# A fused scan and feed-forward kernel: wide decays, low words on ScalarE, scan products in two pieces

## The chip, the cores and the metric

The kernel runs on one core of one Trainium2 chip. The metric is device time in microseconds (us) of that core for one execution. In the profile the core's engines are PE (TensorE, matrix products; PEld is its loading of weights), DVE (VectorE), ACT (ScalarE), POOL (GpSimd) and SP (SyncE, which here issues nearly all DMAs). Each engine has its own list of instructions, and engines wait for each other through semaphores.

## The reference

A Mamba-2 scan is followed by a feed-forward layer with ELU. The scan's inputs are x (4 batches, 8 heads, 768 tokens, 32 channels), a decay `a` per token and head, and B and C (16 states per token and head). Cut to one chunk of tokens, it is:

```python
cum = np.cumsum(np.log(np.clip(a, 1e-06, 1.0)), axis=-1)
L = np.exp(cum[:, :, :, None] - cum[:, :, None, :]) * causal
M = np.einsum('bhin,bhjn->bhij', C, B) * L
y = np.einsum('bhij,bhjd->bhid', M, x) + np.einsum('bhin,bhnd->bhid', C, state) * np.exp(cum)[..., None]
state = np.exp(la.sum(-1))[..., None, None] * state + np.sum(Bx_decayed_to_the_end, axis=2)
```

The 8 heads of 32 channels then stand side by side as 3072 tokens of 256 features, and

```python
h = x @ w_in                      # 256 -> 2048
g = np.where(h > 0.0, h, np.exp(np.minimum(h, 0.0)) - 1.0)
out = g @ w_out                   # 2048 -> 256
```

`w_in` and `w_out` arrive as 64-bit floats. The kernel reads them as pairs of 32-bit words and makes 32-bit floats of them itself, with integer and float operations on the words.

## The kernel before, in words

**Tiling.** The tokens are cut into 12 blocks of 256 tokens (`BLK`), three per batch. A block has two tiles of 128 tokens (u), each of two chunks of 64 (v); the scan works on chunks of 64 instead of 32, which gives the same y. Blocks are counted 0 to 11 in the order of the work; blocks 0 and 1 are the first blocks of two batches, 2 and 3 the next ones of the same batches, and so on.

**The scan of a block.** `spread_cum` (by a DMA that reads each row for 64 partitions) lays the running sums of the log decays into a tile L of 128 x 1024. `decay_of(n, h)` makes the decays of one head of it: two ACT exponentials of 128x64 (line 521), whose bias is a column of `ncum`, minus the running sum of the row's token. After every fourth head two POOL instructions (line 526, `affine_select`) put zeros above the diagonal. `decay(n, q)` is two heads. `scores` makes the products of B and C in four PSUM tiles, `weigh` multiplies one of them by L into M on DVE, `sums` makes the chunks' contributions to the state, `states` runs the recurrence on DVE and spreads each state with its head mask on POOL (Sx). `across` multiplies the states by C into four PSUM tiles y, `inside` adds the products of M and x (line 634), and the results are copied to SBUF as yT (line 651, ACT).

**The words of the weights.** `pieces` 0 to 7 are w_in, 8 to 15 are w_out, each 128x512 32-bit results. `w_take` issues an absolute value of the high word (`w_abs`, ACT, line 196), the low word (`w_low`, line 205 on ACT or 209 on DVE) and the sign (`w_sign`, DVE). `w_give` issues two DVE operations that clip and join (`w_high`, lines 231 and 238) and a POOL sum that puts high and low together (`w_sum`, line 248). Nobody may use the piece before that sum.

**The first layer.** For blocks 0 and 1, and for the first half of the columns of blocks 2 and 3, it is made by `l1` in 32-bit floats (line 666): one PSUM tile for 256 columns, and `elu` evicts it with two ACT instructions (679, 686) and one on DVE (688), which makes g. From block 2's ninth column group on, `l1_words` (line 786) multiplies words instead: y is split into a high word y1, a rest y0 and a combination of both, w likewise (`words_of_w`, `low_of_w` on POOL, `words_of_y`, `both_of_y`). A group of 128 columns of two blocks takes three pairs of products, into a tile `high` and a tile `both`. ACT scales `both` into e (line 790), DVE joins it to `high` (793), `begin_end` makes the exponential on ACT (799, 800) and `end_words` g on DVE (807).

**The second layer.** For blocks 0 and 1 it is `l2` (line 826), which accumulates 16 products of 128 rows in one output tile; from block 2 on it is `second` (line 901), which multiplies two blocks at once with seven products instead of eight, on sums and differences of quarters that POOL and DVE make. `second` is a generator: `l2s(k)` in the schedule issues its next k pieces, of two products each.

**What sets the order.** The kernel runs with a schedule by hand: each engine's instructions stand in the order in which Python issues them. PSUM tiles of the pool "a" come round in a ring of seven, so a product that takes a tile waits until the one seven tiles earlier has been read.

After a start-up for blocks 0 and 1, a loop of twelve steps `s` (from line 1089) makes the first layer of block 1 and the rest of block 0. On the side it makes the decays of block 2 (one head in each of steps 0 to 7, line 1093), a weight piece in each odd step (5 to 10), block 2's turns of B and C, its scores and state products in step 7, block 3's first four heads of decay in step 9 (1125), and block 2's `inside` in step 10.

A second loop of eight steps `j` (from 1170) makes the first layer of blocks 2 and 3 (four tiles each), the second layer of block 0, pieces 11 to 15 (in all steps but 1, so 15 in step 5), the other decays of block 3 (step 0), its scores, states and `inside` (steps 1 to 3), and in step 4 the words of y of blocks 2 and 3.

A third loop of eight (i) goes on with the word products of blocks 2 and 3 and with `l2` of block 1; in its step 4 stand `across` and `inside` of blocks 4 and 5. The last loop takes two blocks at a time (n = 4 to 10): sixteen word products with their share of `second` for the two blocks before, and the scan of the two blocks after, whose `inside` stands at k = 13 and whose words of y stand at k = 15. DMAs of the weights stand on SP's queue in the order of use; the loads of pieces 11 to 15 are issued in the twelve-step loop.

Of the kernel before, what the change touches and what calls it, by code (L numbers as in the profile page):

```python
# [14 lines left out]
ALU = mybir.AluOpType  # L15
ACT = mybir.ActivationFunctionType

P = 128
Q = 64
# [13 lines left out]
def kernel(  # L33
# [73 lines left out]
    def rows_of(n):  # L107
        b, g = place(n)
        return slice(NG * NH * b + g, NG * NH * (b + 1), NG)
# [403 lines left out]
    def decay(n, q):  # L513

        decay_of(n, 2 * q)
        decay_of(n, 2 * q + 1)

    def decay_of(n, h):
        L, row = st[n]["L"], rows_of(n).start + NG * h
        for u in range(2):  # L520
            nc.scalar.activation(  # L521
                L[:, h, u], L[:, h, u], ACT.Exp, bias=ncum[:, u, row:row + 1])
        if h % 4 == 3:
            for v in range(2):
                part = L[Q * v:Q * v + Q, h - 3:h + 1]
                nc.gpsimd.affine_select(  # L526
                    out=part, in_=part, pattern=[[0, 4], [0, 2], [1, Q]],
                    compare_op=ALU.is_ge, fill=0.0, base=0, channel_multiplier=-1)

# [89 lines left out]
                            tile_position=(32 * q, col), skip_group_check=True)  # L621
        return y

    def inside(y, *ns):

        for t in range(2):
            for at, n in enumerate(ns):
                s = st[n]
                for u in range(2):
                    for v in range(2):  # L630
                        toks = slice(Q * v, Q * v + Q)
                        for q in range(4):
                            h, col = 4 * t + q, (D * q + shift(n, v)) % P
                            nc.tensor.matmul(  # L634
                                out=y[t][v][col:col + D, at, u],
                                lhsT=s["x"][toks, u, D * h:D * (h + 1)],
                                rhs=s["M"][h // 2][toks, u, h % 2], start=False, stop=True,
                                tile_position=(Q * v, col), skip_group_check=True)
            n = ns[0]
            if n // 2 not in yT:  # L640
                yT[n // 2] = ffn.tile([P, KC, 2, 2, P], F32, tag="yT", name="yT")
            out = yT[n // 2][:, t, n % 2:n % 2 + len(ns)]
            for v in range(2):
                k = shift(n, v)
                for at in (0, k) if k else (0,):
                    count, src = P - k, (at + k) % P
                    to, src = out[at:at + count, :, :, Q * v:Q * v + Q], y[t][v][src:src + count]
                    if t and n == 1:
                        nc.vector.tensor_copy(to, src)
                    else:  # L650
                        nc.scalar.copy(out=to, in_=src)
        for n in ns:
            st.pop(n)


    g_of = {}
# [92 lines left out]
    def words_of_y(n):  # L749

        y = yT[n // 2].rearrange("p k b u i -> p k (b u i)")
        y1 = conv.tile([P, KC, 2 * BLK], F32R, tag="y1", name="y1", bufs=1)
        y0 = conv.tile([P, KC, 2 * BLK], F32R, tag="y0", name="y0", bufs=1)
        nc.scalar.activation(y1[:, 1], y[:, 1], ACT.Copy, scale=NEAR / WORD)
        if n == 4:
            nc.scalar.activation(y1[:, 0], y[:, 0], ACT.Copy, scale=NEAR / WORD)
        else:
            nc.vector.tensor_scalar(
                out=y1[:, 0], in0=y[:, 0], scalar1=NEAR / WORD, scalar2=None, op0=ALU.mult)
        for k in range(KC):  # L760
            nc.vector.scalar_tensor_tensor(  # L761
                out=y0[:, k], in0=y1[:, k].bitcast(F32), scalar=WORD, in1=y[:, k],
                op0=ALU.mult, op1=ALU.subtract)
        y_words[n] = y1, y0
# [8 lines left out]
                in1=y[:, k], op0=ALU.mult, op1=ALU.add)  # L773
        y_words[n] = y1, y0, both

    def l1_words(n, m):

        cols = slice(m % 2 * P, (m % 2 + 1) * P)
        w, w0 = k_words[m // 2]
        w1, both_w, w0 = w[:, 0, :, cols], w[:, 1, :, cols], w0[:, :, cols]  # L780
        y1, y0, both_y = y_words[n]
        high, both = psum([P, 2 * BLK], "ps_h"), psum([P, 2 * BLK], "ps_w")
        passes = [(high, w1, y1), (high, w0, y0), (both, both_w, both_y)]
        for ps, lhs, rhs in passes if n > 2 and m == 0 else passes[2:] + passes[:2]:
            for k in range(KC):
                nc.tensor.matmul(  # L786
                    out=ps, lhsT=lhs[:, k], rhs=rhs[:, k], start=k == 0 and lhs is not w0,
                    stop=k == KC - 1 and lhs is not w1)
        e = ffn.tile([P, 2 * BLK], F32, tag="e", name="e", bufs=2)
        nc.scalar.activation(e, both, ACT.Copy, scale=WORD)  # L790
        if late:
            end_words()
        nc.vector.scalar_tensor_tensor(  # L793
            out=high, in0=high, scalar=WORD - 1.0, in1=e, op0=ALU.mult, op1=ALU.add)
        late.append((n, m, high, e))
# [167 lines left out]
    def w_take(i, low):  # L963

        w_abs(i)
        w_low(i, low)
        w_sign(i)
# [121 lines left out]
    for s, (n, i) in enumerate((  # L1089
            (1, 0), (1, 1), (1, 2), (0, 4), (1, 3), (0, 5), (1, 4), (0, 6), (1, 5), (0, 7),  # L1090
            (1, 6), (1, 7))):
        l1(n, i, parts=2 if s < 2 else 1)
        if s < 8:
            decay_of(2, s)
        if s == 7:
            st[0] = kept
            scores(2)
            sums(2, 0, pool=p_o, tag="o", parts=(None, last))
            weigh(2, 0)
            weigh(2, 1)  # L1100
        if s % 2 == 1 and todo < 11:
            w_take(todo, nc.vector)
            w_give(todo)
            w_load(todo + 6)
            todo += 1
        if s in (1, 3):
            load_bc(3, us=(s // 2,))
        if s == 9:
            write_flat(0)
        if s == 4:  # L1110
            scaled(2, nc.gpsimd)
        if s == 5:
            turn(2)
            turn_exp(2)
        if s == 4:
            load_x(3)
            spread_exp(3)
        if s == 8:
            weigh(2, 2)
            weigh(2, 3)  # L1120
            states(0, last)
            st.pop(0)
            states(2)
        if s == 9:
            decay(3, 0)
            decay(3, 1)
        if s == 10:
            spread_cum(4)
            inside(across(2), 2)
        if len(lag) > 1:  # L1130
            elu()
# [38 lines left out]
    for j in range(2 * DIRECT):  # L1170
        n, i = 2 + j // DIRECT, j % DIRECT
        if j < 7:
            l2(0, j)
        piece = todo < len(pieces) and j != 1
        if j == 0:
            elu()
        if piece:
            w_take(todo, nc.vector)
        l1(n, i)
        if j == 7:  # L1180
            l2(0, j)
        if j == 0:
            scaled(3, nc.gpsimd)
            turn(3)
            elu()
            turn_exp(3)
        if piece:
            w_give(todo)
            todo += 1
        while lag:  # L1190
            elu()
        if j == 0:
            decay(3, 2)
            decay(3, 3)
        if j == 1:
            scores(3)
            sums(3)
            for q in range(4):
                weigh(3, q)
        if j == 2:  # L1200
            states(3)
        if j == 3:
            inside(across(3), 3)
        if j == 4:
            words_of_y(2)
        if j == 4:
            words_of_w(4)
        if j == 5:
            low_of_w(4)
        if j == 5:  # L1210
            both_of_y(2)
        scan_ahead(j)
        if j == 3:
            s_out[:] = weight_sums()
        if j == 6:
            differences(0, 4)
        if j == 7:
            words_of_w(5)
    for j in range(8, 16):
# [32 lines left out]
        if i == 3:  # L1252
            l2(1, 3)
        if i == 4:
            l2(1, 4)
            y = across(4, 5)
            inside(y, 4, 5)
        if i == 5:
            l2(1, 5)
        if i in (0, 1, 3, 4):  # L1260
# [37 lines left out]
    for n in range(4, NP, 2):  # L1298
# [3 lines left out]
        def l2s(count):  # L1302
            for _ in range(count):
                next(steps)

        for k in range(16):
            l1_words(n, k)
            if m and k == 15:
                words_of_y(m)
            turn_step(n, k // 2 * 2 + 1, k % 2)  # L1310
            if n == 4 and k == 0:
                decay(6, 1)
# [9 lines left out]
            if not m:  # L1322
                l2s(4 if k % 2 else 3)
                continue
            l2s((3 + (n == 4), 3 - (n == 4), 3, 3, 3, 3, 3, 3, 4, 5, 2, 2, 3, 1, 3, 0)[k])
            if k == 9:
                scores(m, m + 1)
                sums(m, m + 1)
# [5 lines left out]
                states(m + 1)  # L1334
            if k == 13:
                y = across(m, m + 1)
                l2s(2)
                inside(y, m, m + 1)
        if m:
            l2s(4)  # L1340
            both_of_y(m)
# [38 lines left out]
```

## Time and profile before

| | |
|---|---|
| three runs | 352.52, 352.54, 353.02 us; median 352.54 |
| the profiled execution | span 351.1 us, 9871 instructions, TensorE clock 1.0 |
| PE | 339.3 us busy (97%) |
| DVE | 259.8 us (74%) |
| ACT | 234.8 us (67%) |
| POOL | 217.2 us (62%) |
| ACT from 30 to 60 us | 9.34, 9.13 and 9.46 of each 10 us |

Of the profiled execution its span is known, from its first to its last instruction; the runs' times also hold what lies around it. Busy shares are means over the whole span, and the stages differ: until 28 us the pipeline fills; from 28 to 83 us stand the loops of twelve and eight steps; from 118 us on the last loop repeats with a period of about 53 us. A row of the timeline gives start, length, engine, line, operation, result and operands, how many instructions were joined to the row, and in brackets how long the engine had been idle and who ended that. A row of a group gives, after its count, busy time and mean length in ns, and the idle time before. PE's lengths are modelled and overlap, so its waits are best seen in the distance from one start to the next.

### The profile page before, as it was taken

How to read it: one execution, taken by the hardware profiler on the slowest of the kernel's cores; microseconds unless marked ns; L12 is line 12 of the kernel's file. 1: busy time of each engine (PE TensorE's matmuls, PEld its weight loads, DVE VectorE, ACT ScalarE, POOL GpSimd, SP SyncE). 2: the span in 40 equal slices, each digit the busy share in tenths (PEclk: the TensorE clock that was granted, in tenths of full speed). 3: DMA queues.
4: the chain of work that ended last, by engine and by line, in shares of the span. 5: the costliest groups of instructions: out<-in, count | busy, mean ns of one | idle time of the engine just before them, and what ended most of it. 6: DMA issues, size and time to landing. Idle time of an engine off the chain costs nothing.

```text
span 351.1 us, 9871 instructions
## 1 busy us (share of the span) xinstructions
PE 339.3 (97%) x3878; PEld 297.3 (85%) x3878; DVE 259.8 (74%) x515; ACT 234.8 (67%) x537; POOL 217.2 (62%) x338
## 2 busy tenths in 40 slices
PE   8789999998999999999999999999999999999995
PEld 5469888887777899988889988889988999999995
DVE  4798988879997899875878775878775766665332
ACT  5688989597748888657599447599457466565000
POOL 5563554566999599975196764196754164455760
PEclk9999999999999999999999999999999999999999
DMA  8887998370270421170421170320000100001002
GB/s 143 220 226 150 315 190 239 89 138 31 65 142 7 94 59 31 12 155 4 106 60 32 13 153 5 93 45 2 2 0 5 62 0 3 0 2 60 3 0 62
DMA packets 72727, 26.49 MB, mean 75 GB/s; under 512 B 57768, under 2 KB 67560, under 8 KB 72680
## 3 DMA queue, kind: packets, MB, share of 16 engines
q1 hardware_dynamic: 70360, 25.60, 31.7%
q8 instruction: 30, 0.49, 0.6%
q10 hardware_dynamic: 2320, 0.26, 0.5%
q14 instruction: 17, 0.14, 0.1%
HBM read 22.51 MB, written 3.34 MB: 74 GB/s over the span
## 4 chain that ended last, share of the span: by engine, by line
PE 82%; SPq 4%; DMA 4%; DVE 3%; POOL 3%; ACT 2%; issue 2%; POOLq 0%; DVEq 0%
PE ps_o L901 35%; PE ps_h L786 18%; PE ps_w L786 9%; PE ps_h L666 8%; PE ps_o L826 4%; PE ps_y L634 2%; DMA w<-in_moe_w_in_dram 2%; DMA xr<-in_x_dram 2%; PE ps_g L541 2%; SPq L178 2%; PE ps_y L616 1%; PE ps_st L571 1%; POOL L L526 1%; POOL w L842 1%; DVE y L761 1%
## 5 line engine op out<-in xcount | busy, mean ns | idle before, releaser
L901 PEld LDWEIGHTS ps_o<-w_out,g 128*128 128x128 f32 x640 | 78.5, 191 | 3.4
L901 PE MATMUL ps_o<-w_out,g 128*128 128x128 f32 x640 | 80.1, 275 | 0.0
L799 ACT ACTIVATE e<-ps_h 128x512 f32<-128x512 f32 x72 | 43.0, 597 | 46.8 <-DVE ps_h L793 46.8
L807 DVE SCALAR_TENSOR_TENSOR g<-e,ps_h 128x512 f32<-128x512 f32 x72 | 49.3, 685 | 32.4 <-ACT e L800 32.1
L842 POOL TENSOR_TENSOR g<-g 128x256 f32<-128x256 f32 x36 | 26.6, 739 | 58.1 <-DVE g L807 58.0
L793 DVE SCALAR_TENSOR_TENSOR ps_h<-ps_h,e 128x512 f32<-128x512 f32 x72 | 50.0, 695 | 12.0 <-ACT e L790 9.1
L790 ACT ACTIVATE e<-ps_w 128x512 f32<-128x512 f32 x72 | 42.3, 587 | 19.8 <-PE ps_w L786 19.7
L786 PE MATMUL ps_w<-y_both,w_words 128*128 128x512 f32 x144 | 52.0, 439 | 0.1
L666 PE MATMUL ps_h<-yT,w_in 128*128 128x256 f32 (+1 forms) x208 | 45.1, 367 | 3.5 <-POOL w_in L248 3.5
L800 ACT ACTIVATE e<-e 128x512 f32<-128x512 f32 x72 | 45.5, 632 | 2.3
L786 PE MATMUL ps_h<-y,w_words 128*128 128x512 f32 x144 | 45.6, 398 | 0.0
L786 PE MATMUL ps_h<-y,w 128*128 128x512 f32 x144 | 44.9, 392 | 0.2 <-POOL w L842 0.2
L666 PEld LDWEIGHTS ps_h<-yT,w_in 128*128 128x128 f32 x208 | 36.3, 190 | 9.4 <-POOL w_in L248 4.6
L521 ACT ACTIVATE L<-L,ncum 128x64 f32<-128x64 f32 x160 | 42.2, 337 | 0.2
L901 PE MATMUL ps_o<-w_sum,g 128*128 128x128 f32 x304 | 38.4, 275 | 0.0
L901 PEld LDWEIGHTS ps_o<-w_sum,g 128*128 128x128 f32 x304 | 37.0, 192 | 1.3 <-ACT e L790 0.2
L526 POOL TENSOR_SCALAR_AFFINE_SELECT L<-L 64x512 f32<-64x512 f32 x40 | 29.3, 733 | 9.6 <-ACT L L521 8.3
L786 PEld LDWEIGHTS ps_h<-y,w 128*128 128x128 f32 x144 | 27.0, 188 | 7.0 <-POOL w L842 0.7
L786 PEld LDWEIGHTS ps_h<-y,w_words 128*128 128x128 f32 x144 | 26.7, 188 | 6.2 <-issue 0.5
L842 POOL TENSOR_TENSOR g<-t,g 128x256 f32<-128x256 f32 x40 | 28.2, 736 | 5.8 <-PE ps_o L901 5.7
L826 PE MATMUL ps_o<-w_out,g 128*128 128x256 f32 x128 | 30.5, 382 | 1.0 <-POOL w_out L248 1.0
L842 POOL TENSOR_TENSOR g<-g,t 128x256 f32<-128x256 f32 x40 | 28.7, 753 | 0.2
(133 smaller groups left out, 536.7 us busy)
## 6 DMA issues: line engine op xcount, KB each, us to landing
L<-flat SPq DMA_DIRECT2D x20, 256.0 KB
w<-in_moe_w_out_dram SPq DMA_DIRECT2D x8, 512.0 KB
w<-in_moe_w_in_dram SPq DMA_DIRECT2D x7, 512.0 KB
xr<-in_x_dram SPq DMA_DIRECT2D x24, 128.0 KB
out_dram<-c_sum SPq DMA_DIRECT2D x9, 256.0 KB
bc<-in_B_dram SPq DMA_DIRECT2D x24, 64.0 KB
bc<-in_C_dram SPq DMA_DIRECT2D x22, 64.0 KB
ec<-flat_exp SPq DMA_DIRECT2D x10, 128.0 KB
```

The lines of the kernel that those rows point to most:

```text
L521: nc.scalar.activation(L[:, h, u], L[:, h, u], ACT.Exp, bias=ncum[:, u, row:row + 1])
L526: nc.gpsimd.affine_select(out=part, in_=part, pattern=[[0, 4], [0, 2], [1, Q]], compare_op=ALU.is_ge, fill=0.0, base=0, channel_multiplier=-1)
L666: nc.tensor.matmul(out=ps[:, j, toks], lhsT=w_in[i][:, k, j * P:(j + 1) * P], rhs=yT[n // 2][:, k, n % 2].rearrange("p u i -> p (u i)")[:, ...
L786: nc.tensor.matmul(out=ps, lhsT=lhs[:, k], rhs=rhs[:, k], start=k == 0 and lhs is not w0, stop=k == KC - 1 and lhs is not w1)
L790: nc.scalar.activation(e, both, ACT.Copy, scale=WORD)
L793: nc.vector.scalar_tensor_tensor(out=high, in0=high, scalar=WORD - 1.0, in1=e, op0=ALU.mult, op1=ALU.add)
L799: nc.scalar.activation(e, high, ACT.Relu, scale=-1.0)
L800: nc.scalar.activation(e, e, ACT.Exp, scale=-1.0)
L807: nc.vector.scalar_tensor_tensor(out=g_of[n, m].rearrange("p b i -> p (b i)"), in0=e, scalar=1.0, in1=h, op0=ALU.subtract, op1=ALU.max)
L826: nc.tensor.matmul(out=o_of[n][:, ts], lhsT=g_of[n, j][:, m % 2, ts * P:(ts + 1) * P], rhs=w_out[:, m], start=(m == 0 and ts == 0), stop=( ...
L842: nc.gpsimd.tensor_tensor(out=out, in0=in0, in1=in1, op=ALU.subtract)
L901: nc.tensor.matmul(out=ps[:, ts], lhsT=b[:, ts * P:(ts + 1) * P], rhs=a[:, i], start=(i == chunk[0] and ts == 0), stop=(i == chunk[-1]), s ...
```

## The change

1. `w_take` makes the low word on ACT, not DVE, for pieces 5 to 15.
2. A new function `decay_half` makes four heads of a block's decays at once: one POOL sum of L and ncum over 128x512, one ACT exponential over 128x512, then the two masks, which now stand in a function `mask`. Blocks 2 and 3 use it: block 2 in steps 2 and 4 of the twelve-step loop, block 3 in step 9 and in step 0 of the eight-step loop. The other blocks keep `decay_of`.
3. Piece 15 moves from step 5 of the eight-step loop to the end of step 4, ahead of the words of y.
4. `words_of_y` makes both halves of y1 on ACT for blocks 2 and 4 (before: for 4 alone). For blocks 2 and 3 the first word group (m = 8) multiplies `high` before `both`. In the last loop the words of y are issued between the products of group 15 and that group's eviction.
5. `inside` can be issued in two pieces, and two or four products of the second layer are put ahead of and between them.

```diff
+    def decay_half(n, half, eng=nc.gpsimd):
+        heads = slice(4 * half, 4 * half + 4)
+        part = st[n]["L"][:, heads]
+        rows = rows_of(n)
+        rows = slice(rows.start + 4 * NG * half, rows.start + 4 * NG * (half + 1), NG)
+        eng.tensor_tensor(
+            out=part, in0=part,
+            in1=ncum[:, :, rows].rearrange("p u h -> p h u").unsqueeze(3).to_broadcast(
+                [P, 4, 2, Q]), op=ALU.add)
+        nc.scalar.activation(part, part, ACT.Exp)
+        mask(n, half)
...
-    def inside(y, *ns):
-        for t in range(2):
+    def inside(y, *ns, ts=(0, 1)):
+        for t in ts:
...
-        if n == 4:
+        if n < 6:
             nc.scalar.activation(y1[:, 0], y[:, 0], ACT.Copy, scale=NEAR / WORD)
...
-        for ps, lhs, rhs in passes if n > 2 and m == 0 else passes[2:] + passes[:2]:
+        for ps, lhs, rhs in passes if m == (8 if n == 2 else 0) else passes[2:] + passes[:2]:
...
+        if between:
+            words_of_y(between)
         e = ffn.tile([P, 2 * BLK], F32, tag="e", name="e", bufs=2)
         nc.scalar.activation(e, both, ACT.Copy, scale=WORD)
...
-        if s < 8:
-            decay_of(2, s)
+        if s in (2, 4):
+            decay_half(2, s // 2 - 1)
...
         if s % 2 == 1 and todo < 11:
-            w_take(todo, nc.vector)
+            w_take(todo, nc.scalar)
...
         if s == 9:
-            decay(3, 0)
-            decay(3, 1)
+            decay_half(3, 0)
...
         if piece:
-            w_take(todo, nc.vector)
+            w_take(todo, nc.scalar)
...
+        if j == 4:
+            w_take(todo, nc.scalar)
+            w_give(todo)
+            todo += 1
         if j == 0:
-            decay(3, 2)
-            decay(3, 3)
+            decay_half(3, 1)
...
         if i == 4:
-            l2(1, 4)
             y = across(4, 5)
-            inside(y, 4, 5)
+            l2(1, 4, half=0)
+            inside(y, 4, 5, ts=(0,))
+            l2(1, 4, half=1)
+            inside(y, 4, 5, ts=(1,))
...
-            l1_words(n, k)
-            if m and k == 15:
-                words_of_y(m)
+            l1_words(n, k, between=m if k == 15 else None)
...
-            l2s((3 + (n == 4), 3 - (n == 4), 3, 3, 3, 3, 3, 3, 4, 5, 2, 2, 3, 1, 3, 0)[k])
+            l2s((3 + (n == 4), 3 - (n == 4), 3, 3, 3, 3, 3, 3, 4, 5, 2, 2, 3, 1, 2, 0)[k])
...
                 y = across(m, m + 1)
+                l2s(1)
+                inside(y, m, m + 1, ts=(0,))
                 l2s(2)
-                inside(y, m, m + 1)
+                inside(y, m, m + 1, ts=(1,))
```

More of the change, by code (lines that the diff above doesn't have):

```diff
@@ L516, in decay, with mask @@
         decay_of(n, 2 * q + 1)
+    def decay_half(n, half, eng=nc.gpsimd):
[9 more added lines that the diff above has]
+        mask(n, half)
+    def mask(n, half):
+        for v in range(2):
+            part = st[n]["L"][Q * v:Q * v + Q, 4 * half:4 * half + 4]
+            nc.gpsimd.affine_select(
+                out=part, in_=part, pattern=[[0, 4], [0, 2], [1, Q]],
+                compare_op=ALU.is_ge, fill=0.0, base=0, channel_multiplier=-1)
     def decay_of(n, h):
@@ L523, in decay_of @@
         if h % 4 == 3:
[L524 to L528, printed above, removed]
+            mask(n, h // 4)
     def scores(*ns):
@@ L651, in inside @@
                         nc.scalar.copy(out=to, in_=src)
-        for n in ns:
-            st.pop(n)
+        if 1 in ts:
+            for n in ns:
+                st.pop(n)
     g_of = {}
@@ L774, in both_of_y, with l1_words @@
         y_words[n] = y1, y0, both
-    def l1_words(n, m):
+    def l1_words(n, m, between=None):
         cols = slice(m % 2 * P, (m % 2 + 1) * P)
```

## The prediction

> **What bounds the kernel now.** I read the page's engine table first, then the chain that ended last, then the table of 10 us windows, then the timeline from 24 to 97 us, where the change has nearly all its edits.
>
> ```profile
> span 351.1 us, 9871 instructions
> PE 339.3 (97%) x3878; PEld 297.3 (85%) x3878; DVE 259.8 (74%) x515; ACT 234.8 (67%) x537; POOL 217.2 (62%) x338
> PE 82%; SPq 4%; DMA 4%; DVE 3%; POOL 3%; ACT 2%; issue 2%; POOLq 0%; DVEq 0%
> ```
>
> The windows (us, length, then PE, PEld, DVE, ACT and POOL busy with their counts, clock, DMA share, GB/s):
>
> ```profile
> 30.00:40.00 10.00, 10.00 (x58) 9.05 (x58) 8.96 (x17) 9.34 (x23) 5.21 (x6) 1.00 0.93 276
> 40.00:50.00 10.00, 9.99 (x168) 8.08 (x173) 9.19 (x23) 9.13 (x24) 5.35 (x9) 1.00 0.94 217
> 50.00:60.00 10.00, 10.00 (x116) 8.53 (x105) 8.31 (x16) 9.46 (x25) 4.61 (x5) 1.00 1.03 262
> ```
>
> TensorE (PE) is the bound: 97% busy, 82% of the chain, full clock. So an engine beside it matters only where PE waits for it, and a wait put on PE stays in the time. Between 30 and 60 us ScalarE (ACT) is busy 9.1 to 9.5 us of 10, GpSimd (POOL) about half. The averages of the whole span (ACT 67%) hide that.
>
> ```profile
> 31.47 0.69 DVE L238 SCALAR_TENSOR_TENSOR mag<-mag,sgn 128x512 uint32<-128x512 uint32 x1
> 32.24 1.27 POOL L248 TENSOR_TENSOR w_in<-mag,w_in 128x512 uint32<-128x512 uint32 x1 [1.79 <-DMA xr<-in_x_dram]
> 32.50 0.57 ACT L679 ACTIVATE e<-ps_h 128x512 f32<-128x512 f32 x1
> ...
> 46.13 2.02 ACT L521 ACTIVATE L<-L,ncum 128x64 f32<-128x64 f32 x8
> 50.37 0.69 DVE L238 SCALAR_TENSOR_TENSOR mag<-mag,sgn 128x512 uint32<-128x512 uint32 x1
> 50.31 1.66 ACT L651 COPY yT<-ps_y 128x128 f32<-128x128 f32 x6 [1.01 <-PE ps_y L634]
> 50.63 1.99 PE L666 MATMUL ps_h<-yT,w_in 128*128 128x256 f32 x8
> 51.14 1.26 POOL L248 TENSOR_TENSOR w_out<-mag,w_out 128x512 uint32<-128x512 uint32 x1 [2.04 <-DVE mag L238]
> 52.35 1.40 POOL L526 TENSOR_SCALAR_AFFINE_SELECT L<-L 64x512 f32<-64x512 f32 x2
> ...
> 83.05 1.99 PE L826 MATMUL ps_o<-w_out,g 128*128 128x256 f32 x8 [1.01 <-POOL w_out L248]
> 105.93 0.74 PE L634 MATMUL ps_y<-M,xr 64*32 64x64 f32 x51 [0.41 <-issue]
> 160.89 0.46 PE L634 MATMUL ps_y<-M,xr 64*32 64x64 f32 x31 [0.32 <-issue]
> ```
>
> See three things. The exponentials of block 3 end on ACT at 48.15, but their mask (L526) starts at 52.35: it stands on POOL behind a weight sum (L248) that waits for DVE's L238. PE takes up the last product of block 1 at 50.63, as soon as ACT has copied the first y out of PSUM (50.31). And PE breaks off inside the scan products (L634) for 0.3 to 0.4 us, with no releaser shown.
>
> **Step 1, low words by ScalarE.** Eleven pieces (5 to 15): DVE loses 11 x 0.43 = 4.7 us, ACT gains 11 x 0.66 = 7.3 (0.67 is the same-sized L196; L205 itself shows 0.75 under overlap; back to back I add 0.6). No PE instruction waits for it directly.
>
> **Step 2, wide decays.** For blocks 2 and 3 ACT loses 32 exponentials at 2.02/8 = 0.25, 8.1 us, and gains four of 128x512 at 0.63 (L686's row), 2.5 us. POOL gains four 128x512 sums L + ncum. No row shows that one: between 0.74 (L842, 128x256) and 1.64 (twice L408's 0.82, a 128x256 sum with a broadcast operand); I take 1.28, L248's, which has its size. Beside step 1, ACT's work from 28 to 57 us is nearly unchanged. But each exponential now waits for its sum on POOL, and each sum stands behind the weight sum just issued, which waits for three DVE operations, of which the first waits for ACT's own absolute value. Behind the waiting exponential on ACT stand the eviction of the next first-layer tile (L679, L686) and the copies of y, and PE waits for these.
>
> A, block 2's first half: L238 ends at 32.16 less a low of 0.6, 31.6; weight sum 32.9, sum 34.2, exponential 34.85. The next eviction starts there, not at 32.50: +2.35. PE has PSUM tiles in hand and does not feel it. B, its second half: eviction, absolute value and low word 37.25, DVE's three 38.1, weight sum 39.4, sum 40.7, exponential 41.3; the eviction that began at 36.33 begins at 41.3. After the copy of the turned B (44.05) and two evictions (45.25, 46.45), DVE ends its two products g at 46.25 and 47.1. Scores and state products of block 2 reuse those PSUM tiles: state products start at 47.1, not 43.34, **+3.8**.
>
> C, block 3's first half: in the trace L238 ends 7.7 us after the state products began (51.06 - 43.34); less two lows (0.8) that is 54.0 now. Weight sum 55.3, sum 56.6, exponential 57.2, eviction 58.4, first copy of y 58.7. PE's product of 50.63 needs the tile which that copy frees: +8.1 so far, so **C is 4.3**. D, its second half, ACT after the copies (59.95): the 6.2 us that it takes from 51.97 to 58.15, plus two lows, 67.35; DVE's g, C-scale, clip and join to 69.5 (rows 0.69, 0.41, 0.41, 0.69); weight sum 70.8, sum 72.1, exponential 72.75, eviction 74.0, g 74.7. The first-layer product that starts at 62.60 reuses that tile: +12.1, **D is 4.0**. From there to block 3's across product PE is bound by itself again (-0.2).
>
> [...] If queues let later work pass, the sum would be without A to D, 349.2.
>
> SP's order is unchanged, but its reload of the decay buffer for block 4 waits for block 2's products M, some 4 us later than now, with that block's other loads behind it; it is issued at 54.29 now, its first reader runs 10 us later and is late by D too: 0.
>
> **Step 3, piece 15 earlier.** Its absolute value, low word, three DVE operations and weight sum move ahead of the words of y; its load is issued where it was, SP's order is unchanged, and POOL takes the sum ahead of a mask. The wait at 83.05 (start to start 1.17 above its neighbours) goes: **-1.2**. What is late next is the copy that frees the output tile, behind 2.6 us more ACT work (lows, first half of y): +0.55; the 0.75 us that PE waits for a low word near 92 goes, since its mask and sums come earlier: **-0.2** together.
>
> **Step 4, words of y.** Block 2: ACT +0.62, DVE -0.71 (L754, L758), and the product of both words goes last; no PE wait stands there now, so 0. The later groups issue the words before the last eviction; DVE does the same work in another order, and both halves end with y_both, behind a sum that waits for PE: 0, between -0.3 and +0.3 each (a y_both wait of 0.42 on the loads is what the trace has), three times.
>
> **Step 5, scan products in two pieces.** Start to start, the four breaks in L634 are 0.62, 0.53, 0.47 and 0.70 us. They fall after 78 or 97 products, not at the seam of 64, and each ends 2.4 to 3.1 us after the start of a packet of the page's q8 (instruction, 30 packets in 0.49 MB, 16 KB each; the trace has them at 102.85, 158.45, 211.45 and 264.33): I take them for instruction supply. Four to six ordinary products between the pieces give it time: 0.86 us at the first (four of 0.216), all 0.6 gained; 0.45 more than now at the other three (four of 0.11): **-0.6 - 1.35**. Between 0 (another cause) and -2.3.
>
> [...]
>
> **Sum.** 3.8 + 4.3 + 4.0 - 0.2 - 1.2 - 0.2 - 0.6 - 1.35 = +8.55 on the profiled 351.1: span 359.65. The median of the runs, 352.54, is 1.4 above that span (what lies around it): **361.0 us**.
>
> **Rivals.**
> Faster: the seven PSUM tiles let PE run ahead of ACT at all four waits, as at A. Then only steps 3 and 5 count, -1.4 and -1.95: 349.2. It decides from the point where A to D cost PE under 3.35 together. For it: 30 to 40 us, no PE idle while ACT trails by a tile. Against: PE starts within 0.3 us of ACT's copy at 50.31. 0.07 (0.05 clearly faster, 0.02 near no change).
> Block 2 absorbed: B costs nothing because the turned tiles come free in time; C and D remain: 361.0 - 3.8 = 357.2. For it: ACT's queue before 40 us has slack I can't see. 0.23.
> ACT stays behind: the 2.6 us more ACT work from 57 to 80 us comes through whole, 363.6. For it: ACT 9.9 of 10 us from 70 to 80. Against: it idles 3.7 of 10 from 60 to 70. 0.13.
> Breaks stay: step 5 gives nothing, 363.0. 0.09.
> Forecast: 0.48.
>
> **The range.** The sum on POOL moves all four waits: at 0.74 it is 4 x 0.54 less, 358.8; at 1.64, 1.4 more, 362.4. With step 4's +-0.9 and the two neighbours it is 355.5 to 364.5; the likeliest alone 358.0 to 363.5. Under 0.2% (0.7 us) a change of this kernel can't be told from none. Faster 0.05, same 0.02, slower 0.93.
>
> **What would show it.** In the changed kernel ACT idles 2 to 5 us before each of the four 128x512 exponentials, released by POOL's new sum; PE idles about 4 us ahead of the last first-layer product of block 1 and of the third of block 2; ACT busy falls below 8 of 10 between 30 and 75 us. The wait for w_out at the last second-layer product of block 0 is gone, and L634's breaks are gone or under 0.3. I am wrong if ACT's exponentials start without a wait, or if they wait and PE has no idle time beside them.

## The result, and the profile after

The changed kernel takes 363.31 us (median of four runs, 362.92 to 363.87), the kernel before 352.61 us beside it (352.52 to 353.02): a ratio of 1.0298, 95% interval 1.028 to 1.0317, **10.7 us slower**. The forecast was 361.0 with a range of 355.5 to 364.5, so the side and the range hold, and 2.3 us are missing from the sum.

The page after: the span, the table of engines, the granted clock of TensorE in 40 slices, and the chain that ended last.

```profile
span 361.8 us, 9853 instructions
PE 347.3 (96%) x3878; PEld 302.4 (84%) x3878; DVE 252.3 (70%) x503; ACT 236.5 (65%) x521; POOL 221.3 (61%) x342
PEclk9999968989999999999999999999999999999999
PE 71%; ACT 8%; POOL 7%; DVE 6%; issue 3%; SPq 2%; DMA 2%; POOLq 0%; DVEq 0%; ACTq 0%
```

Nothing but PE looks like a bound in the first two lines. The last line tells more: PE fell from 82% of the chain to 71%, while ACT, POOL and DVE rose from 2, 3 and 3% to 8, 7 and 6%. So another 13% of the span now runs over the three other engines. The clock line has a dent from its sixth slice on that the kernel before does not have.

The timeline after, ACT's four wide exponentials and what ended ACT's idle time ahead of each:

```profile
33.96 0.63 ACT L528 ACTIVATE L<-L 128x512 f32<-128x512 f32 x1 [2.70 <-POOL L L524]
40.34 0.63 ACT L528 ACTIVATE L<-L 128x512 f32<-128x512 f32 x1 [2.23 <-POOL L L524]
56.62 0.63 ACT L528 ACTIVATE L<-L 128x512 f32<-128x512 f32 x1 [6.00 <-POOL L L524]
72.16 0.63 ACT L528 ACTIVATE L<-L 128x512 f32<-128x512 f32 x1 [4.64 <-POOL L L524]
```

ACT stands still for 15.6 us in front of 2.5 us of work, as A to D of step 2 had it. POOL itself shows why the sum comes so late (timeline after, around the third one):

```profile
54.31 1.26 POOL L248 TENSOR_TENSOR w_out<-mag,w_out 128x512 uint32<-128x512 uint32 x1 [1.77 <-DVE mag L238]
55.53 1.05 POOL L524 TENSOR_TENSOR L<-L,ncum 128x512 f32<-128x512 f32 x1
```

The sum takes 1.05 us and waits for nothing of its own; it starts when the weight sum ahead of it in POOL's order ends, and that one was waiting for DVE. PE then waits for what stands behind the exponential on ACT (timeline after):

```profile
45.25 1.98 PE L557 MATMUL ps_g<-ctm,bct 32*64 32x128 f32 x32 [2.78 <-ACT e L696]
47.15 0.90 PE L587 MATMUL ps_st<-xr,sc 64*32 64x64 f32 x40
...
58.60 3.56 PE L683 MATMUL ps_h<-yT,w_in 128*128 128x256 f32 x8 [1.95 <-ACT yT L667]
...
74.77 2.68 PE L683 MATMUL ps_h<-yT,w_in 128*128 128x256 f32 x8 [2.13 <-DVE g L705]
77.24 2.94 PE L845 MATMUL ps_o<-w_out,g 128*128 128x256 f32 x8
80.01 1.89 PE L683 MATMUL ps_h<-yT,w_in 128*128 128x256 f32 x8
```

Before, the same instructions start without a wait (timeline before; the one between them, at 50.63, stands in the prediction):

```profile
42.71 0.69 PE L541 MATMUL ps_g<-ctm,bct 32*64 32x128 f32 x32
43.34 0.66 PE L571 MATMUL ps_st<-xr,sc 64*32 64x64 f32 x40
...
62.81 1.89 PE L666 MATMUL ps_h<-yT,w_in 128*128 128x256 f32 x8
```

In the changed kernel, eight products of 128x256 take 1.89 us in the last row, but 3.56, 2.68 and 2.94 in the rows just after a stall. The windows after (length, then busy time of PE, PEld, DVE, ACT, POOL with counts, granted clock, DMA share, GB/s) say it in another way:

```profile
40.00:50.00 10.00, 7.22 (x89) 5.50 (x88) 7.17 (x15) 9.50 (x18) 3.95 (x6) 0.76 0.80 180
50.00:60.00 10.00, 8.05 (x121) 6.46 (x120) 4.68 (x13) 3.86 (x11) 5.93 (x10) 0.84 0.86 248
60.00:70.00 10.00, 10.00 (x74) 8.39 (x72) 6.50 (x12) 7.38 (x13) 2.02 (x3) 0.89 0.33 64
70.00:80.00 10.00, 7.87 (x77) 6.15 (x59) 4.54 (x11) 5.43 (x12) 4.98 (x6) 0.83 0.50 106
```

The clock was 1.00 in all four before; the last two were:

```profile
60.00:70.00 10.00, 9.99 (x193) 8.30 (x194) 8.39 (x21) 6.31 (x16) 5.31 (x9) 1.00 0.37 78
70.00:80.00 10.00, 10.00 (x48) 8.81 (x47) 8.07 (x13) 9.86 (x31) 5.72 (x6) 1.00 0.68 126
```

PE's 10.00 between 60 and 70 us after the change is no sign of health: its products are long there because the clock is 0.89. This was not in the forecast.

### The profile page after: what moved, and what is told of

It is laid out like the page before. It is cut to its first block, busy times and chain, and to the rows that moved or that the text cites. A ratio compares the mean times of both kernels' runs of the same rounds, so it can differ in the third digit from the quotient of the medians.

```text
span 361.8 us, 9853 instructions
## 1 busy us (share of the span) xinstructions
PE 347.3 (96%) x3878; PEld 302.4 (84%) x3878; DVE 252.3 (70%) x503; ACT 236.5 (65%) x521; POOL 221.3 (61%) x342
## 4 chain that ended last, share of the span: by engine, by line
PE 71%; ACT 8%; POOL 7%; DVE 6%; issue 3%; SPq 2%; DMA 2%; POOLq 0%; DVEq 0%; ACTq 0%
PE ps_o L920 35%; PE ps_h L803 17%; PE ps_w L803 9%; PE ps_o L845 3%; PE ps_y L650 2%; ACT e L696 2%; DMA w<-in_moe_w_in_dram 2%; POOL L L534 2%; PE ps_h L683 2%; ACT e L703 2%; PE ps_g L557 2%; POOL w_out L248 1%; DVE mag L238 1%; PE ps_y L632 1%; POOL L L524 1%
## 5 line engine op out<-in xcount | busy, mean ns | idle before, releaser
L826 DVE SCALAR_TENSOR_TENSOR g<-e,ps_h 128x512 f32<-128x512 f32 x72 | 49.4, 686 | 31.0 <-ACT e L819 30.7
L683 PE MATMUL ps_h<-yT,w_in 128*128 128x256 f32 (+1 forms) x208 | 49.5, 393 | 6.7 <-DVE g L705 2.1
L683 PEld LDWEIGHTS ps_h<-yT,w_in 128*128 128x128 f32 x208 | 38.9, 203 | 14.1 <-POOL w_in L248 3.9
L534 POOL TENSOR_SCALAR_AFFINE_SELECT L<-L 64x512 f32<-64x512 f32 x40 | 30.3, 759 | 11.7 <-ACT L L541 7.4
L541 ACT ACTIVATE L<-L,ncum 128x64 f32<-128x64 f32 x128 | 33.7, 337 | 0.0
L705 DVE SCALAR_TENSOR_TENSOR g<-e,ps_h 128x512 f32<-128x512 f32 x24 | 16.4, 684 | 22.9 <-ACT e L703 22.8
L845 PE MATMUL ps_o<-w_out,g 128*128 128x256 f32 x128 | 32.1, 395 | 0.0
```

What stands on the lines that cost most here:

```text
L534: nc.gpsimd.affine_select(out=part, in_=part, pattern=[[0, 4], [0, 2], [1, Q]], compare_op=ALU.is_ge, fill=0.0, base=0, channel_multiplier=-1)
L541: nc.scalar.activation(L[:, h, u], L[:, h, u], ACT.Exp, bias=ncum[:, u, row:row + 1])
L683: nc.tensor.matmul(out=ps[:, j, toks], lhsT=w_in[i][:, k, j * P:(j + 1) * P], rhs=yT[n // 2][:, k, n % 2].rearrange("p u i -> p (u i)")[:, ...
L826: nc.vector.scalar_tensor_tensor(out=g_of[n, m].rearrange("p b i -> p (b i)"), in0=e, scalar=1.0, in1=h, op0=ALU.subtract, op1=ALU.max)
L845: nc.tensor.matmul(out=o_of[n][:, ts], lhsT=g_of[n, j][:, m % 2, ts * P:(ts + 1) * P], rhs=w_out[:, m], start=(m == 0 and ts == 0), stop=( ...
```

## The experiments

Theory: the wide decays cost the time, by the place of their sums in POOL's order; the rest of the change gains a little. The medians of the kernel before were 352.63 to 352.84 us beside the runs below; differences are from the ratio and its interval.

### The wide decays taken out, and put in alone

In the first, the decays of blocks two and three go back; in the second, they alone are added to the kernel before.

```diff
-        if s in (2, 4):
-            decay_half(2, s // 2 - 1)
+        if s < 8:
+            decay_of(2, s)
...
-            decay_half(3, 0)
+            decay(3, 0)
+            decay(3, 1)
...
-            decay_half(3, 1)
+            decay(3, 2)
+            decay(3, 3)
```

> The changed kernel with the decays of blocks two and three taken back to one ScalarE instruction for each head and half, as before; the other four parts of the change stay. Theory (the wide decays' sums on POOL make ScalarE late, and everything else in the change saves a little): 349.5 to 351.0 us, with TensorE's granted clock 1.00 from 40 to 80 us and none of the waits of 2 to 3 us on TensorE in that stretch. Rival (the low words and words of y that went to ScalarE make it late by themselves): 354 to 358 us, with waits of TensorE on ScalarE between 40 and 80 us.

> The kernel before with the wide decays of blocks two and three and nothing else of the change. Theory (four ScalarE waits for POOL's sums, then products at a lower granted clock after each stall of TensorE): 364.5 to 367 us, with waits of some 15 us of ScalarE on the POOL sums and a granted clock of 0.76 to 0.9 between 40 and 80 us. Rival (the loss needs the low words on ScalarE beside them): 355 to 360 us.

Without them: 351.80 us, ratio 0.9971 (0.9955 to 0.9988), 1.0 us faster than before. With them alone: 366.73 us, 1.0404 (1.0368 to 1.0439), 14.3 us slower (13.0 to 15.5). Both rivals fall, and the pair settles the place: the wide decays are all of the loss. The second run is slower still than the whole change. ACT waits longer in it (timeline of the run with the wide decays alone):

```profile
35.17 0.63 ACT L528 ACTIVATE L<-L 128x512 f32<-128x512 f32 x1 [3.05 <-POOL L L524]
41.86 0.63 ACT L528 ACTIVATE L<-L 128x512 f32<-128x512 f32 x1 [3.20 <-POOL L L524]
58.61 0.63 ACT L528 ACTIVATE L<-L 128x512 f32<-128x512 f32 x1 [7.68 <-POOL L L524]
73.15 0.63 ACT L528 ACTIVATE L<-L 128x512 f32<-128x512 f32 x1 [5.08 <-POOL L L524]
```

They add up to 19.0 us instead of 15.6. In this kernel the low word is again a DVE operation ahead of the weight sum, which would make the POOL sum behind that later; the pair of wide decays and low words alone was not run. But PE does not pay for the longer waits. Counted from the products ahead of block two's scores (the first-layer row at 39.16 us in the profile before, 39.80 here and 38.85 in the changed kernel), the last eight 32-bit products of the first layer of blocks two and three start 13.8 us late in this run and 13.7 in the changed kernel. Behind it the changed kernel wins back 1.6 us, and this run loses another 0.6; that fits steps 3 to 5, which it lacks.

The run without the wide decays gained less than the 3.35 us that the other parts were to bring, and stays above the theory's range. In its trace the part from that first-layer row to PE's last product is even 0.7 us longer than before; there the gain comes from a start-up 0.9 us and an end 1.1 us shorter. Its timeline shows a new wait of PE, ahead of block two's state products, that the kernel before does not have:

```profile
43.58 0.65 PE L587 MATMUL ps_st<-xr,sc 64*32 64x64 f32 x40 [1.06 <-issue]
```

### The same work, the POOL sums earlier

The wide form stays, but `decay_half` is cut in two: `decay_sum` holds its POOL sum, the rest its exponential and masks. The sums are issued one loop step or more before their exponentials.

```diff
+        if s == 1:
+            decay_sum(2, 0)
+            decay_sum(2, 1)
+        if s == 8:
+            decay_sum(3, 0)
+            decay_sum(3, 1)
         if s in (2, 4):
             decay_half(2, s // 2 - 1)
```

> The changed kernel with the four POOL sums of the wide decays issued ahead: both of block two in the step s=1 (in place of s=2 and s=4), both of block three in s=8 (in place of s=9 and j=0); the four exponentials and the masks stay in their places. Theory (it is the place of the sum in POOL's queue just ahead of its reader, and not the wide form, that costs): ScalarE's waits on the sums fall from 15.6 us to under 3 us, the granted clock is 1.00 from 40 to 80 us, 349 to 351.5 us. Rival (the wide form itself costs, since every product of the scan waits for half a block of decays at once and POOL's queue is later by the sums anyway): 356 to 362 us.

352.11 us, ratio 0.9985 (0.997 to 1.0001): one of ACT's four waits on the sums is left, with 1.28 us, the clock is 1.00, and 11.2 us of the changed kernel's 363.31 come off with the same instructions. It is the order that cost the time, not the operation. What is left is in the timeline of this run (ACT, then PE):

```profile
47.39 0.63 ACT L531 ACTIVATE L<-L 128x512 f32<-128x512 f32 x1 [1.28 <-POOL L L524]
50.02 0.71 PE L635 MATMUL ps_y<-bct,Sx 32*64 32x64 f32 x32 [1.33 <-POOL Sx L612]
```

The sums of block three now stand ahead of the masked states (Sx) in POOL's order, and PE waits for those.

> The changed kernel with the two POOL sums of block two alone issued ahead, in s=1; those of block three stay in s=9 and j=0. Theory of the prediction (C and D, at s=9 and j=0, are 8.3 us of their own on top of what A and B had cost): 360 to 361.5 us, that is 8 to 9 us above the run with all four sums early. Rival (one chain: the place where the sums of block three stop ScalarE is set by POOL's queue, and the delay of block two would have been hidden behind it): 362.3 to 363.5 us, no gain. Second rival (C and D came only from a ScalarE that A and B had made late): below 356 us.

The edit leaves block three's sums in steps s=9 and j=0 and moves only block two's. It takes 359.62 us, ratio 1.019 (1.017 to 1.021): 7.5 us (by the medians) above the run with all four early, where the prediction had 8.3 for C and D, and 3.7 us below the changed kernel, where it had 3.8 for A and B. That is a little less than the theory's range, and the first rival falls. The second rival falls too: the waits of block three are their own (timeline, ACT then PE):

```profile
52.54 0.63 ACT L531 ACTIVATE L<-L 128x512 f32<-128x512 f32 x1 [6.22 <-POOL L L524]
68.62 0.63 ACT L531 ACTIVATE L<-L 128x512 f32<-128x512 f32 x1 [4.65 <-POOL L L524]
```

```profile
54.52 3.78 PE L686 MATMUL ps_h<-yT,w_in 128*128 128x256 f32 x8 [4.14 <-ACT yT L670]
71.23 1.99 PE L686 MATMUL ps_h<-yT,w_in 128*128 128x256 f32 x8 [2.15 <-DVE g L708]
```

> All of the change, with the POOL sums of block two in s=1 and those of block three in s=6. In the run with the latter in s=8, POOL stood idle for 3.2 us until 45.1 and TensorE then waited 1.33 and 0.60 us for the masked states that stood behind the sums. Theory (the sums now lie in the idle stretch and the waits of TensorE for the masked states go): 350.3 to 351.5 us. Rival (the two waits were not on the path that sets the end, or the low words on ScalarE set it): 351.8 to 352.5 us, as with s=8.

With block three's sums in s=6 in place of s=8: 350.91 us, ratio 0.9961 (0.9939 to 0.9984). The wait of 1.33 us is gone and the products behind it start 1.4 us earlier than with s=8; a wait of 0.60 us near 68 us stays. There was a price on the other side that I had not reckoned (POOL's timeline):

```profile
43.79 2.74 POOL L524 TENSOR_TENSOR L<-L,ncum 128x512 f32<-128x512 f32 x2 [2.20 <-DMA L<-flat]
```

The first of the two sums now waits for the DMA that lays out L. Here most of this falls into a stretch in which POOL had waited for DVE anyway (3.21 us with s=8).

> As the run with the sums of block three in s=6, and the low words of pieces five to fifteen on VectorE as before the change. Theory (the low words on ScalarE cost 0.4 to 1.0 us, and all parts that gain add up): 349.8 to 351.0 us. Rival (with ScalarE relieved by the wide exponentials the low words cost nothing there, and VectorE is no better place): within 0.4 us of the run with the low words on ScalarE.

351.77 us, ratio 0.9974 (0.9958 to 0.9991), 0.9 us above the run with the low words on ACT, with intervals that overlap, and in the range of neither theory nor rival: by the times, which engine is better once the sums are early stays open. The traces, one of each, lean to ACT: from the first-layer row at 39.16 us to the last first-layer product of block one PE loses 2.6 us against the kernel before with the low words on DVE, and 0.4 with them on ACT.

### The other parts, one at a time

Each is the kernel before with this part alone.

```diff
# low words
-            w_take(todo, nc.vector)
+            w_take(todo, nc.scalar)
# piece fifteen
+        if j == 4:
+            w_take(todo, nc.vector)
+            w_give(todo)
+            todo += 1
# two pieces (first of four places)
-            l2(1, 4)
             y = across(4, 5)
-            inside(y, 4, 5)
+            l2(1, 4, half=0)
+            inside(y, 4, 5, ts=(0,))
+            l2(1, 4, half=1)
+            inside(y, 4, 5, ts=(1,))
```

> The kernel before with the low words of the pieces five to fifteen on ScalarE and nothing else of the change. Theory of the prediction (step 1 costs TensorE nothing): within 0.3 us of the kernel before. Rival (read from the trace of the run without wide decays, where TensorE lost 2.0 us between 42 and 67 us against the kernel before: there ScalarE has both the 32 small exponentials and the low words, and it is late): 1.0 to 2.0 us slower than before, lost between 42 and 67 us.

353.03 us, ratio 1.0023 (1.0002 to 1.0044): 0.8 us slower, between 0.1 and 1.6. The rival is nearer; from the first-layer row at 39.16 us to PE's last product its trace is 1.4 us longer than before. The trace has the same wait of 1.06 us ahead of block two's state products as the run without wide decays.

> The kernel before with the last piece of w_out (piece 15) made at the end of the step j=4 and nothing else of the change (its low words stay on VectorE). Theory of the prediction (step 3 takes away the wait of 1.2 us near 70 us): 1.0 to 1.4 us faster than before. Rival (the gain is given back where the next chain off TensorE stands, by the words of y): less than 0.4 us faster.

351.71 us, ratio 0.9974 (0.9962 to 0.9986): 0.9 us faster (0.5 to 1.3), near the theory; between the same two points its trace is 1.0 us shorter.

> The kernel before with the scan products in two pieces, a half or one of the second layer's steps between them, and nothing else of the change. Theory of the prediction (step 5 hides the breaks of supply in the dense small products): 1.5 to 2.3 us faster than before. Rival (as in the trace of the run without wide decays, where the first place gave nothing and the later ones some 0.3 us each): 0.5 to 1.2 us faster. Second rival (the breaks only move): no difference.

351.68 us, ratio 0.9974 (0.9956 to 0.9992): 0.9 us faster (0.3 to 1.6); the first rival. The breaks became smaller without vanishing, as at the second place (0.20 us of idle time, 0.32 before; timeline; the first row is one piece, the last two are the other, with the break in it):

```profile
157.62 0.86 PE L634 MATMUL ps_y<-M,xr 64*32 64x64 f32 x64
158.41 1.16 PE L902 MATMUL ps_o<-w_sum,g 128*128 128x128 f32 x8
159.50 0.44 PE L634 MATMUL ps_y<-M,xr 64*32 64x64 f32 x29
160.14 0.56 PE L634 MATMUL ps_y<-M,xr 64*32 64x64 f32 x35 [0.20 <-issue]
```

Yet the trace does not show where the gain lies: the same product comes 1.37 us earlier than before at 98 us, ahead of the first place, and 1.06 earlier at the end. What speaks for a gain are the medians; its mechanism stays open.

> The kernel before with piece fifteen earlier, the order of the words of y and the scan products in two pieces: no wide decays, no low words on ScalarE. Theory (the two parts that were each 0.9 us faster alone add up, the words of y cost nothing): 350.5 to 351.2 us. Rival (both remove the same delay or the gains are given back): 351.5 to 352.2 us.

350.66 us, ratio 0.9943 (0.9927 to 0.996): 2.0 us faster (1.4 to 2.6), where the two gains measured alone add up to 1.8. By the medians they add, and the words of y cost nothing that shows; the trace agrees, with 2.1 us less between these two points. But 1.1 us of that lie at the three later places of the scan products, where the run with the two pieces alone is 0.2 us later than before. The words of y (step 4) were not run alone, so which of steps 4 and 5 gains there stays open. The run beats both kernels and has the lowest median of all that was run; the interval of the run with the sums in s=1 and s=6 overlaps with its own.

### The clock after a stall

Products of the identity with zeros are put ahead of the three stalls of the changed kernel. The second run has three, two and two.

```diff
+    def fill(count, out=None):
+        first = out is None
+        if first:
+            out = p_o.tile([P, 4, P], F32, tag="o", name="ps_fill")
+        for _ in range(count):
+            nc.tensor.matmul(
+                out=out, lhsT=ident, rhs=zeros.unsqueeze(2).to_broadcast([P, 4, P]),
+                start=first, stop=first, skip_group_check=True)
...
+            fill(5)
             scores(2)
...
+        if s == 11:
+            fill(4)
         l1(n, i, parts=2 if s < 2 else 1)
...
+        if j == 2:
+            fill(4, o_of[0].rearrange("p u (a i) -> p (u a) i", i=P))
         l1(n, i)
```

> The changed kernel with products of the identity with zeros (128x512, into the idle bank or added as zero to the sum of the second layer) put ahead of the three instructions at which TensorE stood still for 2.9, 2.2 and 2.3 us: five ahead of the scores of block two, four ahead of the last first-layer product of block one, four ahead of the third of block two. Theory (the half-speed products after each stall come from TensorE's own idleness): granted clock 1.00 from 40 to 80 us, the products behind the stalls at 0.216 us instead of 0.426, and, since what came after the third stall was not hidden, 361.3 to 362.4 us. Rival (the half speed comes from something else that happens there, a neighbour's load or the long waits of ScalarE): clock and time unchanged, 363.0 to 364.0 us.

> As the run with filling products, but three, two and two of them in place of five, four and four (one takes 0.89 us, not the 0.45 on which the first counts were based, so the first filling ran 2.1 us and the third 0.8 us past the end of the wait). Theory (half-speed products cost what is not hidden, and the first run lost its gain to the overlong fillings and to a break of supply of 1.16 us at 117 us): granted clock 1.00, the third first-layer product of block two ends and what follows comes 1.0 to 1.6 us earlier than in the changed kernel, 361.6 to 362.6 us. Rival (a delay of TensorE there is hidden or given back later whatever its size): 363.0 to 363.8 us.

The first takes 363.50 us, ratio 1.0316 (1.0287 to 1.0346), the second 363.04, 1.0295 (1.0265 to 1.0325). In both the granted clock is 1.00 between 40 and 80 us. The windows and the third stall of the second run:

```profile
40.00:50.00 10.00, 9.66 (x102) 6.67 (x101) 7.43 (x15) 9.28 (x17) 4.41 (x6) 1.00 1.04 216
70.00:80.00 10.00, 8.09 (x51) 5.80 (x57) 5.51 (x15) 6.42 (x14) 5.61 (x9) 1.00 0.57 115
```

```profile
74.44 1.99 PE L695 MATMUL ps_h<-yT,w_in 128*128 128x256 f32 x8 [1.91 <-DVE g L717]
76.27 1.89 PE L857 MATMUL ps_o<-w_out,g 128*128 128x256 f32 x8
78.00 1.89 PE L695 MATMUL ps_h<-yT,w_in 128*128 128x256 f32 x8
```

From the first of these rows to the third it is 3.56 us, and 5.24 in the changed kernel (74.77 to 80.01): half speed cost 1.7 us there. So this much is shown: with work on PE in the time of the stalls the clock stayed at 1.00 in both runs, where the changed kernel has 0.76 to 0.89. What that is worth in time is not shown. Both medians lie in the rivals' ranges, and the intervals overlap with that of the changed kernel. In the traces the part between these two points is 1.1 and 1.3 us shorter than in the changed kernel, although 0.6 us are given back by a break near 117 us.

## Why the prediction was right, and where its sum was off

**Step 2, right in its chain, and with some luck in its times.** State products of block two were forecast at 47.1 and start at 47.15; the last first-layer product of block one at +8.1 (58.7) and comes at 58.60; the third of block two at +12.1 (74.7), at 74.77. PE did not feel A, as said. For block three the chain was what the forecast had: its exponentials were to end at 57.2 and 72.75 and end at 57.25 and 72.79. The POOL sum, bounded by 0.74 and 1.64 and taken as 1.28, measures 1.05, but the weight sums ahead of it end 0.3 us later than forecast (55.57 and 71.11). What was to show it wrong, exponentials without waits, did not come.

The luck: these are times from the start of the span, and the start-up ran 0.31 us ahead of the one before (the first-layer row at 39.16 us comes at 38.85), which hides as much of each delay. At 47.15 PE does not wait for the tile that was named, since DVE is done with both g at 46.69, before the 47.1 of the forecast:

```profile
45.35 1.34 DVE L705 SCALAR_TENSOR_TENSOR g<-e,ps_h 128x512 f32<-128x512 f32 x2
```

It is the scores ahead, 1.98 us long at half clock instead of 0.69, that reach to 47.1. And the 62.60 from which D was counted is the start of the product's weight load; the product itself starts at 62.81, so its delay is 11.96 and not 12.1. Two signs came out otherwise: PE idles 1.95 and 2.13 us ahead of those two products, not about 4, because products before them ran at half speed (0.426 us from start to start instead of 0.216), and ACT is busy for 9.50 of 10 us between 40 and 50 us.

The run with block two's sums early speaks against the rival in which block two is absorbed (its sums are worth 3.7 us), and the changed kernel's three waits of PE against the one in which the PSUM tiles hide all of them. The rival in which ACT stays behind comes out near the measured time, but not by its mechanism: behind the third stall PE waits for ACT no more, it is slow by its clock (0.50 from 75.9 to 79.3 us). Queues that let later work pass (349.2 in the prediction) are not what the runs show: the POOL sum at 55.53 starts as the weight sum ahead of it ends, and two orders of the same instructions are 11.2 us apart.

**The term after D was mis-sized: -0.2 forecast, +1.46 traced.** The delay is 11.96 us at 74.77 and 13.42 at 93.6, because of the half-speed products. I had priced a stall at its length and not at the clock behind it.

**Step 1 was wrong as a cost of nothing by itself** (0.8 us alone, 0.1 to 1.6), where ACT holds the 32 small exponentials as well; beside the wide decays ACT's waits are shorter with it, without a gain for PE that the traces show by the end of the eight-step loop.

**Step 3 was over-sized:** -1.4 forecast, -0.9 alone. In the changed kernel the delay falls from 13.42 to 12.28 when the wait for w_out is gone (-1.1, near the -1.2), but the low-word wait near 92 us, whose end was to bring 0.75, is still there at 105.3, and the delay is 12.63 behind it.

**Step 5 was over-sized:** -1.95 forecast, -0.9 alone. In the changed kernel the first place brings nothing (12.63 before, 12.86 behind) and the three later ones 1.0 together (11.84 at the end). I had taken each break as won in full; the rival in which the breaks stay was half right: in the changed kernel three of the four are left, at 0.31 to 0.34 us from start to start. That the breaks come from instruction supply was my estimate from the times of the packets; no run shows it.

**Step 4** stands at 0, as far as the sum of the medians can tell; it was not run alone.

Put together by the trace of the changed kernel, at PE's products: 11.96 + 1.46 - 0.79 + 0.23 - 1.02 = 11.84, where the sum had 8.55. From the end of the last write's issue to the end of the span it is then 2.1 us and not 3.2, which takes 1.1 off: 10.7, as the span and the medians have it. Without this and the 0.3 us of the start-up the forecast would have been 3.6 us short, and the time, by this trace, just outside its range.

## What to carry to other kernels

An operation moved to another engine inherits that engine's order (11.2 us here): before handing a sum to an idle-looking queue, look at what stands just ahead of it and what that waits for, and issue it where its operands are there and the queue is free, some steps before its reader. The merged exponentials, which save ACT 5.6 us, were worth nothing that shows with their sums early (350.91 and 352.11 us with them, 351.80 without), since ACT is not the bound, and alone, with their input late, cost 14.3 us. Price a stall of PE with the slower products after it (1.46 us here), and price a removed break by less than its length (0.9 us of 1.95 here).

## What the runs showed that I had not expected

**The clock.** With stalls of PE of 2.78, 1.95 and 2.13 us, the granted clock of the changed kernel is 0.50 from 45.2 to 52.0, from 58.9 to 62.3 and from 75.9 to 79.3 us; 128x256 products then follow each other by 0.426 us instead of 0.216. At the third stall the half speed begins only 1.2 us after the stall has ended. The length of a stall does not decide it alone: after 2.15 us the run with block two's sums early, after 2.16 and 1.91 us the second filled run, and after 3.21 us near 60.6 us the run with the wide decays alone go on at full speed (clock 1.00 in the 10 us window behind each).

What decides beside the length was not shown: no run moved a stall on purpose.

**The ends of the trace.** The start-up, whose instructions are the same in all these kernels, brought the same first-layer product at 34.20 us in the profile before, and between 32.8 and 34.8 in the runs of this study; the end of the span came 3.2 us after the last write's issue before and 2.1 us after the change. The time that lies around the span, 1.4 us in the forecast, is 2.0 to 2.1 us in the four runs of the changed kernel. Differences of traces under 1 us are therefore read between two products in the middle, and not from spans.
